# The first batch pair's loads, tail block and bias in a hand-scheduled attention and MLP-mixer kernel

## The chip, the cores and the metric

The kernel runs on one core of a Trainium2 chip. The metric is device microseconds of one execution; less is better. The core's TensorE (PE, with its weight loads PEld), VectorE (DVE), ScalarE (ACT), GpSimd (POOL) and SyncE (SP) run side by side, each its own instructions in order, and wait for each other by semaphores. Sixteen DMA engines move data; POOL, SP and ACT issue the transfers.

## What is computed

For 8 batches, 8 heads, 576 positions and a head width of 64:

```python
scores = (q @ k.T) / 8 - slopes[h] * abs(i - j)         # masked unless 0 <= i - j < 128
x      = softmax(scores) @ v                            # heads side by side: (8, 576, 512)
h      = relu(x.T @ w_tok1) @ w_tok2                    # 576 -> 256 -> 576, over positions
u      = x + h.T
out    = u + relu(u @ w_ch1) @ w_ch2                    # 512 -> 1536 -> 512, over channels
```

All arrays are float32 in memory. The kernel works in bf16 with float32 sums; the POOL loads convert on the way.

## The kernel before

**Blocks and pairs.** The 576 positions of a batch are 4 blocks of 128 and a rest of 64 (R). Batches go in pairs. A pair has 9 blocks: 0 to 3 are the first batch, 4 to 7 the second, and block 8 (TAIL) holds both rests, the first batch's in partitions 0 to 63 and the second's in 64 to 127. Because of the window of 128 a block looks only at itself and the block before it.

**Stages.** `side(b)` does batch b's attention and its token mixing. For each block: `transposes` (q and k of a block to `qkT`, on PE by L644 with a copy by L650, or later in the kernel as a DMA transpose by L633), `scores` (L684; then exp on ACT, L707; then the product with a mask on DVE, L717), `values` (L750; then reciprocal L763 and normalization L766). Then `token_mix`: L795 and L805 (the tail's share) into relu (L813), L838/L841 back to positions, the sum `ub` (L853, L856), and its transpose `uT` (L873 with copy L879, or a DMA transpose). `main(b)` does the channel mixing: `chunk` (L1035: one of 12 pieces of the hidden width, four matmuls of 512 columns, then relu L1041), `tail_piece` (L1078), and the second product. In every batch `second` (L1212) forms that product by seven half-sized products, which share three accumulation banks: products 1, 6, 7, 4 in one bank, 5 and 3 in another, 2 in the third. Product 6 waits until the result of 1 has been taken out of the bank (L1183), 7 until that of 6, 4 until that of 7, and 3 until that of 5. The tail block's second product is L1123. `main(b)` is interleaved with `side(b+1)`.

**Bias.** Two ways to bring in the slope term and the mask exist. For a block listed in `BIASED` (and of the first pair's first batch) PE adds them before the scores: `bias` (L693), two groups of four matmuls with a diagonal matrix `slant`, 128 columns wide for block 0 and 256 for others. Then DVE does not multiply by a mask. All other blocks use the mask products (L717), two to a block. `TURNED` makes the bias of a block other than 0 wait for that block's transposes.

**What sets the order.** The program is straight-line. `Plan` holds every operation with an engine, a cost and a rank, and `Plan.run` plays them through a model at build time; each engine then gets its operations in the order that came out, once and for all. `SEEDS[part]` adds a random shift of up to 1500 to the ranks of one part (part 0 is the first `side`, part b+1 is `main(b)` with `side(b+1)`); zero leaves the ranks as they are. `HALF` is a rate of the model alone. With `SECOND_LATE` the first matmuls of products 1, 2 and 5 may not be placed before the last scores of the interleaved `side`. `emit` fills PE's planned gaps in the first 60 us with matmuls of zeros (L1268), whose results nobody reads. Nothing of this runs on the chip but its order.

**Loads.** Block 0's q and k come by SP and ACT (L484). All others of the first pair and all weights are issued by POOL in the order of the string `LOADS`: `q2` is q of block 2, `W1` is w_tok1 with the first copy of its rest, `P0` the second copy of that rest, `W2` and `T0` are w_tok2, `A0` to `A3` are quarters of w_ch1 (hidden pieces 0-2, 3-5, 6-8, 9-11), `B0` to `B3` quarters of w_ch2. `load` issues one DMA for a block (128 rows by 8 heads) and, for the tail, one of 64 rows by 8 heads for each batch. A model of eight slots limits how many are under way. The later pairs' loads follow in the order of use; they wait for a free `qk` or `v` buffer (five of each).

**The tail of the first pair.** `q8`, `k8` and `v8` load only the first batch's 64 rows; the other 64 rows of these buffers are zeroed beforehand by L542 and L543. The second batch's rows come later as `lk8`, `lq8` and `lv8`, which rewrite the lower half (`rewrites`, `later`, `slot`): they wait for the first users of the buffer. `side` therefore transposes the tail twice in the first pair, once for each batch.

**Start of the first channel mixing.** In `main(0)` the first `PIECES` pieces of the hidden width are formed block by block (L1020, four matmuls of 128 columns for each block and piece), so that they can begin before all blocks of `uT` are there. Each piece holds a PSUM bank of the four that transposes, values and token mixing use as well.

Of the kernel before, what the change touches and what calls it, by code (L numbers as in the profile page):

```python
# [20 lines left out]
class Buf:  # L21
    def __init__(self, ring, choice):
        self.ring, self.choice, self.slot = ring, choice, None
        self.writers, self.parts, self.users, self.later = [], {}, [], []

    def __call__(self):
        got = self.ring.slots[self.slot[0]]
# [38 lines left out]
class Plan:  # L66
# [6 lines left out]
    def buf(self, name, choice=None):  # L73
        return Buf(self.rings[name], choice or self.rings[name].each)

    def op(self, eng, cost, emit, rank, makes=(), adds=(), rewrites=(), part=None, uses=(), reads=(), needs=(),
           after=0.0, order=None, bus=0.0, other=None, mode=0, behind=()):
        def many(x):
            return list(x) if isinstance(x, (list, tuple)) else [x]

        o = Op()
        o.eng, o.cost, o.emit, o.rank, o.after, o.part = eng, cost, emit, rank, after, self.part
        o.t0 = o.done = None
        o.order, o.bus, o.other, o.mode = order, bus, other, mode
        o.n = len(self.ops)
        o.deps = set(many(needs))
        o.behind = list(behind)
        o.bufs = []
        for b in many(makes):
            b.writers.append(o)  # L90
            o.bufs.append(b)
        for b in many(adds):
            o.deps.update(b.writers)
            b.writers.append(o)
            o.bufs.append(b)
        for b in many(rewrites):
            o.deps.update(u for u in b.users if u not in b.later)
            b.later.append(o)
            b.writers.append(o)
            o.bufs.append(b)  # L100
        if part is not None:
            b, key = part
            b.parts.setdefault(key, []).append(o)
            o.bufs.append(b)
        for b in many(uses):
            o.deps.update(b.writers)
            o.bufs.append(b)
        for b, key in many(reads):
            o.deps.update(b.parts[key])
            o.bufs.append(b)  # L110
        o.deps.discard(o)
        for b in o.bufs:
            b.users.append(o)
        self.ops.append(o)
        return o

    def slot(self):
        self.orders += 1
        return self.orders

    def dma(self, emit, descs, packets, makes=(), rewrites=(), order=None, uses=()):
        o = self.op("POOL", 550 + 0.33 * descs, emit, 0, makes=makes, rewrites=rewrites, uses=uses,
                    order=order or self.slot())
        o.packets = packets
        return o

    def run(self):
        ops = self.ops
        dice = [random.Random(x) for x in SEEDS]
        for o in ops:  # L130
            if SEEDS[o.part]:
                o.rank += dice[o.part].uniform(-SHIFT, SHIFT)
# [177 lines left out]
    def emit(self, spin):  # L310
# [12 lines left out]
        for _, _, go in sorted(work, key=lambda w: w[:2]):  # L323
# [3 lines left out]
WARM = 6500.0  # L327
FIRST = -5e5
GRACE = 0.4
PIECES = 2  # L330
HOLD = 3
FROM_QK = 10
FROM_U = 2
# [4 lines left out]
MERGEM = 9  # L338
MERGES = 9
FAST = range(8)  # L340
PRODUCTS = [1, 5, 6, 2, 3, 7, 4]
RANKT = 0
RANKS = 0
RANKH = 0
RELU = 350
SUMS_AT = 60e3
SEEDS = [63488, 544433, 0, 603260, 673561, 0, 172207, 0, 0]
SHIFT = 1500.0
UNIT_LATE = True
SECOND_LATE = False  # L350
BIASED = [0, 1, 2]
THIRD = [(4, 5)]
TURNED = False
SLANT = 4.0e3
HALVED = 2
BANKS = 8
# [6 lines left out]
STORE = 774.0  # L363
TURN = [(792.0, 1267.0), (1380.0, 2400.0)]
RATES = [(0.37, 0.23), (0.52, 0.35), (0.47, 0.18)]
HALF = 0.7
EARLY = 1


LOADS = ("q2 k1 q1 v1 k2 k3 v0 q3 v2 v8 W1 q8 k8 v3 W2 k6 k5 q5 k4 q6 A0 q4 "  # L370
         "v4 lk8 lq8 k7 A1 q7 v5 A2 B0 v6 A3 v7 lv8 B1 B2 T0 P0 B3")


@with_exitstack
def kernel(
# [16 lines left out]
    P = nc.NUM_PARTITIONS  # L392
    B, H, S, D = q.shape
# [5 lines left out]
    R = S - NC * P  # L399
    NB = 2 * NC + 1  # L400
    TAIL = 2 * NC
# [16 lines left out]
    plan = Plan()  # L418
# [36 lines left out]
    W1 = const.tile([P, NC, DTOK], BF16, name="W1")  # L455
    W1p = const.tile([P, 2, DTOK], BF16, name="W1p")
    W2 = const.tile([P, NJ, NC * P], BF16, name="W2")
# [12 lines left out]
    def rows(t, b, s0, n):  # L470
        return t[b, :, s0 : s0 + n, :].rearrange("h s d -> s h d")

    def parts_of(pr, blk):
        if blk == TAIL:
            return [(2 * pr + i, NC * P, R, i * R) for i in range(2)]
        return [(2 * pr + blk // NC, (blk % NC) * P, P, 0)]

    pe_, act_, dve_ = nc.tensor, nc.scalar, nc.vector
# [27 lines left out]
    def block(pr, blk):  # L506
        if (pr, blk) not in held:
            held[pr, blk] = {"qk": plan.buf("qk"), "v": plan.buf("v")}
        return held[pr, blk]

    def load(name, pr, blk, parts, order=None):
        got = block(pr, blk)
        buf = got["v" if name == "v" else "qk"]
        src = {"q": q, "k": k, "v": v}[name]

        def to():
            return buf()[:, :, 0:D] if name == "v" else buf()[:, "qk".index(name), :, :]

        for b, s0, n, p0 in parts:
            def go(b=b, s0=s0, n=n, p0=p0):  # L520
                nc.gpsimd.dma_start(out=to()[p0 : p0 + n, :, :], in_=rows(src, b, s0, n))  # L521
            kw = {"makes": buf} if order is None else {"rewrites": buf, "order": order}
            plan.dma(go, n * H, 1024 if n == P else 520, **kw)

    def weights(parts):
        return [plan.dma(lambda o=o, i=i: nc.gpsimd.dma_start(out=o, in_=i), n, s) for o, i, n, s in parts]
# [6 lines left out]
    for i_, name in enumerate("qk"):  # L533
        raw = raws[i_]
        buf = block(0, 0)["qk"]
        plan.op("DVE", 480, lambda raw=raw, buf=buf, i="qk".index(name): dve_.tensor_copy(
            out=buf()[:, i, :, :], in_=raw.rearrange("p (h d) -> p h d", h=H)), -100 + i_, makes=buf, after=4.75e3 + 600 * i_)
    if PADT:
        for i in range(2):
            plan.op("DVE", 190, lambda i=i: dve_.memset(W1p[(1 - i) * R : (2 - i) * R, i, :], 0.0), -90)  # L540
    last = block(0, TAIL)
    plan.op("DVE", 180, lambda b=last["qk"]: dve_.memset(b()[R:P, :, :, :], 0.0), -90, makes=last["qk"])  # L542
    plan.op("DVE", 180, lambda b=last["v"]: dve_.memset(b()[R:P, :, 0:D], 0.0), -90, makes=last["v"])  # L543
    lw1, lw2, lw2t, lc1, lc2, later = [], [], [], [], [], []
    for item in LOADS.split():
        what, n = item[:-1], int(item[-1])
        if what in ("q", "k", "v"):
            load(what, 0, n, parts_of(0, n)[0:1])
        elif what in ("lq", "lk", "lv"):
            later.append((what[1], plan.slot()))  # L550
        elif what == "W":
            if n == 1:
                lw1 += weights([(W1[:, 0:NC, :], w1, 512, 2080)] +
                               [(W1p[0:R, 0, :], moe_w_tok1[NC * P : S, :], 64, 420)])
            else:
                lw2 += weights([(W2[:, :, :], w2[:, :, 0 : NC * P], 256, 2630)])
        elif what == "P":
            lw1 += weights([(W1p[R:P, 1, :], moe_w_tok1[NC * P : S, :], 64, 420)])
        elif what == "T":
            lw2t += weights([(W2t[:, :, :], w2[:, :, NC * P : S], 256, 300)])  # L560
        elif what == "A":
            hs = slice(n * DCH // 4, (n + 1) * DCH // 4)
            lc1 += weights([(WC1[:, :, hs], c1[:, :, hs], 512, 2500)]) * (NHT // 4)
        else:
            js = slice(n * NHT // 4, (n + 1) * NHT // 4)
            lc2 += weights([(WC2[:, js, :], c2[:, js, :], 384, 2680)]) * (NHT // 4)
# [52 lines left out]
    qkT, xbs, ubs, r1s, uts, wides = {}, {}, {}, {}, {}, []  # L619
# [267 lines left out]
    def side(b, rank):  # L887
        pr, half = b // 2, b % 2
        if half == 0:
            xbs[pr], ubs[pr] = plan.buf("xb"), plan.buf("ub")  # L890
        if pr < HALVED:
            units = list(range(half * NC, (half + 1) * NC)) + [TAIL]
        else:
            units = [[0, 1, 2, 3, TAIL], [4, 5, 6, 7]][half]
        prev = None
        for u in units + [None]:
            if u is not None:
                need = [u, 2 * NC - 1] if u == TAIL and pr >= HALVED else [u]
                for w in need:
                    if (pr, w) not in qkT or (u == TAIL and pr == 0):  # L900
                        transposes(pr, w, rank(0 if by_transfer(pr, w) else 450))
                hf = half if u == TAIL and pr < HALVED else None
                pb = scores(pr, u, hf, rank(450), wides if b == 1 else ())
            if prev is not None:
                values(pr, prev[0], prev[1], prev[2], rank)
            prev = None if u is None else (u, hf, pb)
        token_mix(b, rank)
# [99 lines left out]
    def main(b, rank):  # L1007
# [6 lines left out]
        if b == 0:  # L1014
            first = [bank() for _ in range(PIECES)]
            for blk in blocks:
# [132 lines left out]
    def second(b, rank, r2, ss, sums, ub):  # L1149
# [53 lines left out]
        DONE = {1: (0, 0, False), 5: (1, 1, False), 6: (0, 1, False), 7: (1, 1, True), 2: (0, 0, True), 3: (0, 1, True), 4: (1, 0, True)}  # L1203
        for m in PRODUCTS:
            l, w, s, tt = L[m]
# [39 lines left out]
    SIDE = [[5 * 930 + 5 * 480, 5 * 930 + 5 * 480], [5 * 930 + 6 * 450, 4 * 930 + 3 * 450]]  # L1245
    base = 0.0
    side(0, along(-1e6, 1.0, 1.0))
    for name, order in later:
        load(name, 0, TAIL, parts_of(0, TAIL)[1:2], order)
    for b in range(B):  # L1250
        n = LEN[b % 2]
        plan.part = b + 1
# [49 lines left out]
```

## Time and profile before

| what | value |
|---|---|
| median of 3 runs (279.9 to 280.82) | 280.22 us |
| profiled execution | 280.18 us |
| its span, first to last instruction | 278.0 us |
| PE busy in the span | 270.4 us, 2871 matmuls |
| DVE, ACT, POOL busy | 210.0, 136.2, 116.3 us |
| matmuls of zeros L1268 | 73, the last at 24.6 us |
| bias matmuls L693 | 24 (8 of 128 columns, 16 of 256), 3.6 to 11.7 us |
| transposes by PE L644 | 88 matmuls, 5.7 to 56.4 us |
| POOL issues of q, k, v L521 | 118, about 0.88 us each for 128 rows |
| granted TensorE clock | 1.00 throughout |

The span is the profile's own clock; 2.2 us of the execution lie around it. Of a matmul the profile shows a modelled end, so that neighbours overlap and a busy PE says little; the distance from start to start is what counts, and the chain of waits shows it: it books each group of matmuls until the next one starts. "x8" after a line is the number of instructions of a group, and what stands in brackets is how long the engine was idle before it and what ended that. For a POOL load the duration is the issuing; "DMA to landing" runs from the start of the issue until the data is there.

### The profile page before, as it was taken

Reading aid. Unit: us, or ns where it says so; the run is one execution under the profiler, and the core shown is the slowest. Engines: PE = TensorE matmul, PEld = TensorE weight load, DVE = VectorE, ACT = ScalarE, POOL = GpSimd, SP = SyncE. Lnnn points to the kernel's source line nnn. Section 1 sums busy time; section 2 is a strip of 40 time slices with the busy share of each in tenths; the row PEclk is TensorE's granted clock in tenths of the full one; section 3 lists DMA queues with packets and bytes.
Section 4 is the critical chain, followed back from the end, with each engine's and each line's share of the span. In section 5 each row is a group of like instructions: output and inputs, shape, how many; then the busy total and the mean of one; then the engine's idle time right before and its main releaser. Section 6 shows DMA issues by size and latency. Waiting matters only on the chain.

```text
span 278.0 us, 7069 instructions
## 1 busy us (share of the span) xinstructions
PE 270.4 (97%) x2871; PEld 181.7 (65%) x2871; DVE 210.0 (76%) x486; ACT 136.2 (49%) x216; POOL 116.3 (42%) x146
## 2 busy tenths in 40 slices
PE   7989999999999999999999999999999999999994
PEld 4865755676686546595667655586666755489983
DVE  8467799968897569964898469862978569877972
ACT  5563996336970298007860087206951077215500
POOL 8998848940382018900594008800480320022000
PEclk9999999999999999999999999999999999999999
DMA  9999999999599689999999999979799930052014
GB/s 132 151 159 170 191 191 179 156 140 232 73 127 154 137 211 128 132 136 202 174 137 158 201 174 75 146 123 207 136 135 112 171 134 2 8 142 98 2 59 130
DMA packets 167535, 38.43 MB, mean 138 GB/s; under 512 B 155792, under 2 KB 166672, under 8 KB 167504
## 3 DMA queue, kind: packets, MB, share of 16 engines
q0 software_dynamic: 116112, 20.03, 92.5%
q1 hardware_dynamic: 50352, 17.70, 31.6%
q8 instruction: 22, 0.36, 0.5%
q10 hardware_dynamic: 1040, 0.26, 0.4%
q14 instruction: 9, 0.07, 0.1%
HBM read 35.85 MB, written 9.44 MB: 163 GB/s over the span
## 4 chain that ended last, share of the span: by engine, by line
PE 85%; DVE 6%; POOL 4%; DMA 2%; issue 0%; ACT 0%; POOLq 0%
PE ps L1212 25%; PE ps L1035 24%; PE ps L750 6%; PE ps L684 6%; PE ps L838 4%; PE ps L795 4%; PE ps L1078 4%; PE ps L1123 4%; PE ps L957 3%; POOL qk L521 2%; DMA v<-in_v_dram 2%; DVE s L1060 1%; POOL v L521 1%; PE ps L644 1%; DVE WT L582 1%; PE ps L873 1%
## 5 line engine op out<-in xcount | busy, mean ns | idle before, releaser
L1035 PE MATMUL ps<-uT,WC 128*128 128x512 bf16 x328 | 79.5, 379 | 0.0
L1041 ACT ACTIVATE r<-ps 128x512 bf16<-128x512 f32 x75 | 44.3, 602 | 57.4 <-PE ps L1035 52.9
L707 ACT ACTIVATE pe<-ps 128x1024 bf16<-128x1024 f32 (+1 forms) x76 | 63.5, 888 | 18.1 <-PE ps L684 17.7
L521 POOL DMA_DIRECT2D v<-in_v_dram x40 | 34.4, 862 | 89.9 <-PE ps L750 88.2
L1035 PEld LDWEIGHTS <-WC 128*128 128x128 bf16 x328 | 29.1, 98 | 28.3
L717 DVE TENSOR_TENSOR pe<-pe,mask 128x1024 bf16<-128x1024 bf16 (+1 forms) x62 | 37.1, 607 | 8.0 <-ACT pe L707 7.3
L1212 PEld LDWEIGHTS <-r 128*128 128x128 bf16 x384 | 36.9, 98 | 7.9 <-issue 0.7
L521 POOL DMA_DIRECT2D qk<-in_q_dram x39 | 34.0, 877 | 2.8 <-PE ps L750 1.4
L521 POOL DMA_DIRECT2D qk<-in_k_dram x39 | 34.1, 883 | 2.1 <-DMA v<-in_v_dram 1.1
L1212 PEld LDWEIGHTS <-s 128*128 128x128 bf16 x288 | 27.5, 98 | 6.3 <-issue 1.8
L766 DVE TENSOR_TENSOR xb<-ps,rt 128x256 bf16<-128x256 f32 (+1 forms) x73 | 29.5, 419 | 0.8
L750 PEld LDWEIGHTS <-pe 128*128 128x128 bf16 (+1 forms) x560 | 21.6, 100 | 9.6 <-DVE pe L717 2.6
L750 PE MATMUL ps<-v,pe 128*128 128x65 bf16 (+1 forms) x560 | 26.2, 194 | 1.2 <-DMA v<-in_v_dram 1.2
L1212 PE MATMUL ps<-WC,r 128*128 128x256 bf16 x192 | 25.4, 273 | 0.0
L1212 PE MATMUL ps<-WT,s 128*128 128x256 bf16 x192 | 24.2, 273 | 0.0
L1212 PE MATMUL ps<-WT,r 128*128 128x256 bf16 x192 | 23.7, 273 | 0.0
L1183 DVE TENSOR_TENSOR ob<-ps,ub 128x512 f32<-128x512 f32 x22 | 15.2, 689 | 10.1 <-PE ps L1212 10.0
L856 DVE TENSOR_TENSOR ub<-ps,xb 128x512 bf16<-128x512 f32 x34 | 21.4, 684 | 1.4 <-PE ps L838 1.2
L684 PEld LDWEIGHTS <-qkT 64*128 64x128 bf16 x560 | 14.8, 94 | 10.9 <-issue 9.7
L763 DVE RECIPROCAL rt<-ps 128x4 f32<-128x4 f32 (+1 forms) x76 | 12.3, 175 | 10.1 <-PE ps L750 9.4
L684 PE MATMUL ps<-qkT 64*128 64x128 bf16 (+1 forms) x304 | 19.4, 216 | 0.0
L838 PE MATMUL ps<-r,W 128*128 128x512 bf16 x64 | 16.1, 379 | 0.1
(96 smaller groups left out, 336.4 us busy)
## 6 DMA issues: line engine op xcount, KB each, us to landing
out_dram<-ob SPq DMA_DIRECT2D x17, 256.0 KB, 2.5
v<-in_v_dram POOLq DMA_DIRECT2D x32, 128.0 KB, 4.8
qk<-in_q_dram POOLq DMA_DIRECT2D x31, 128.0 KB, 4.9
qk<-in_k_dram POOLq DMA_DIRECT2D x31, 128.0 KB, 4.8
WC<-in_moe_w_ch_dram POOLq DMA_DIRECT2D x8, 384.0 KB, 9.0
out_dram<-raw SPq DMA_DIRECT2D x7, 256.0 KB, 2.6
out_dram<-ob POOLq DMA_DIRECT2D x5, 256.0 KB, 2.9
out_dram<-raw POOLq DMA_DIRECT2D x3, 256.0 KB, 3.0
```

The lines of the kernel that those rows point to most:

```text
L521: nc.gpsimd.dma_start(out=to()[p0 : p0 + n, :, :], in_=rows(src, b, s0, n))
L684: pe_.matmul(wide(e)[:, i, kind, a:z], lhsT=ts[kb]()[e * D : (e + 1) * D, NHP + i, :], rhs=ts[blk]()[e * D : (e + 1) * D, i, a:z], start=n ...
L707: act_.activation(out=pb()[:, e, :, lo:, c0:c1_], in_=wide(e)[:, :, lo:, c0:c1_], func=ACT.Exp, scale=scale)
L717: dve_.tensor_tensor(out=o, in0=o, in1=heads(mk, es), op=ALU.mult)
L750: pe_.matmul(view()[a:z, at, i, :], lhsT=pb()[:, e, i, kind, a:z], rhs=vb()[:, h, 0 : D + 1], start=m == 0, stop=m == len(mms) - 1, skip_g ...
L766: dve_.tensor_tensor(out=x4(), in0=view()[r0:r1_, :, :, 0:D], in1=rt()[r0:r1_, 0:n, :, :].broadcast_to([r1_ - r0, n, 4, D]), op=ALU.mult)
L838: pe_.matmul(ht()[:, hs], lhsT=W2[:, j, c * P : (c + 1) * P], rhs=r1()[:, j, :], start=j == 0, stop=j == NJ - 1 and not fold)
L856: plan.op("DVE", 690, lambda blk=blk, ht=ht, hs=hs: dve_.tensor_tensor(out=ub()[:, blk, :], in0=ht()[:, hs], in1=xb()[:, blk, :], op=ALU.a ...
L1035: pe_.matmul(ct()[:, :], lhsT=WC1[:, cb, t * P : (t + 1) * P], rhs=uT()[:, cb, :], start=cb == 0, stop=cb == NCB - 1)
L1041: plan.op("ACT", 600, lambda t=t, ct=ct: act_.activation(out=r2()[:, t, :], in_=ct()[:, :], func=ACT.Relu), rk, part=(r2, t), uses=[ct], o ...
L1183: dve_.tensor_tensor(out=v, in0=bk().rearrange("p (c n) -> p c n", c=2), in1=src, op=ALU.add)
L1212: pe_.matmul(bk()[:, c * HN : (c + 1) * HN], lhsT=l(t, c), rhs=w(t), start=first, stop=g == 1 and t == HK - 1, skip_group_check=True)
```

## The change

The second batch's half of the first pair's tail is no longer loaded apart: `q8`, `k8` and `v8` each issue both halves, one behind the other. The memsets, the rewriting loads and the second transposing of the tail go. PE forms the bias of block 0 only; blocks 1 and 2 are masked by DVE. The first-pair loads and the weights are issued in another order. Three instead of two pieces of the hidden width are begun block by block. In the second product 7 comes before 3, in all batches. `SECOND_LATE` and `TURNED` are switched on, `HALF` is another number, and other parts have their ranks shifted.

```diff
-    def op(..., makes=(), adds=(), rewrites=(), part=None, ...):
+    def op(..., makes=(), adds=(), part=None, ...):
...
-        for b in many(rewrites):
-            o.deps.update(u for u in b.users if u not in b.later)
-            b.later.append(o)
-            b.writers.append(o)
-            o.bufs.append(b)
...
-PIECES = 2
+PIECES = 3
...
-PRODUCTS = [1, 5, 6, 2, 3, 7, 4]
+PRODUCTS = [1, 5, 6, 2, 7, 3, 4]
...
-SEEDS = [63488, 544433, 0, 603260, 673561, 0, 172207, 0, 0]
+SEEDS = [554399, 0, 0, 0, 0, 0, 0, 0, 399558]
...
-SECOND_LATE = False
-BIASED = [0, 1, 2]
+SECOND_LATE = True
+BIASED = [0]
...
-TURNED = False
+TURNED = True
...
-HALF = 0.7
+HALF = 0.9
...
-LOADS = ("q2 k1 q1 v1 k2 k3 v0 q3 v2 v8 W1 q8 k8 v3 W2 k6 k5 q5 k4 q6 A0 q4 "
-         "v4 lk8 lq8 k7 A1 q7 v5 A2 B0 v6 A3 v7 lv8 B1 B2 T0 P0 B3")
+LOADS = ("v0 k1 q1 v1 q3 q2 k2 W1 k3 v2 q8 k8 k5 v3 v8 W2 k6 q6 A0 q5 k4 q4 "
+         "A1 A2 q7 k7 v6 v5 P0 v4 B0 T0 A3 v7 B1 B2 B3")
...
-    last = block(0, TAIL)
-    plan.op("DVE", 180, lambda b=last["qk"]: dve_.memset(b()[R:P, :, :, :], 0.0), -90, makes=last["qk"])
-    plan.op("DVE", 180, lambda b=last["v"]: dve_.memset(b()[R:P, :, 0:D], 0.0), -90, makes=last["v"])
...
         if what in ("q", "k", "v"):
-            load(what, 0, n, parts_of(0, n)[0:1])
-        elif what in ("lq", "lk", "lv"):
-            later.append((what[1], plan.slot()))
+            load(what, 0, n, parts_of(0, n))
...
-                    if (pr, w) not in qkT or (u == TAIL and pr == 0):
+                    if (pr, w) not in qkT:
                         transposes(pr, w, rank(0 if by_transfer(pr, w) else 450))
...
-    for name, order in later:
-        load(name, 0, TAIL, parts_of(0, TAIL)[1:2], order)
```

More of the change, by code (lines that the diff above doesn't have):

```diff
@@ L23, in __init__ @@
         self.ring, self.choice, self.slot = ring, choice, None
-        self.writers, self.parts, self.users, self.later = [], {}, [], []
+        self.writers, self.parts, self.users = [], {}, []
     def __call__(self):
@@ L74, in buf, with op @@
         return Buf(self.rings[name], choice or self.rings[name].each)
-    def op(self, eng, cost, emit, rank, makes=(), adds=(), rewrites=(), part=None, uses=(), reads=(), needs=(),
+    def op(self, eng, cost, emit, rank, makes=(), adds=(), part=None, uses=(), reads=(), needs=(),
            after=0.0, order=None, bus=0.0, other=None, mode=0, behind=()):
@@ L115, in op, with dma @@
         return o
-    def slot(self):
+    def dma(self, emit, descs, packets, makes=(), uses=()):
         self.orders += 1
[L119 to L123, printed above, removed]
+        o = self.op("POOL", 550 + 0.33 * descs, emit, 0, makes=makes, uses=uses, order=self.orders)
         o.packets = packets
@@ L509, in block, with load @@
         return held[pr, blk]
-    def load(name, pr, blk, parts, order=None):
+    def load(name, pr, blk, parts):
         got = block(pr, blk)
@@ L521, in go @@
                 nc.gpsimd.dma_start(out=to()[p0 : p0 + n, :, :], in_=rows(src, b, s0, n))
-            kw = {"makes": buf} if order is None else {"rewrites": buf, "order": order}
-            plan.dma(go, n * H, 1024 if n == P else 520, **kw)
+            plan.dma(go, n * H, 1024 if n == P else 520, makes=buf)
     def weights(parts):
@@ L540 @@
             plan.op("DVE", 190, lambda i=i: dve_.memset(W1p[(1 - i) * R : (2 - i) * R, i, :], 0.0), -90)
-    last = block(0, TAIL)
-    plan.op("DVE", 180, lambda b=last["qk"]: dve_.memset(b()[R:P, :, :, :], 0.0), -90, makes=last["qk"])
-    plan.op("DVE", 180, lambda b=last["v"]: dve_.memset(b()[R:P, :, 0:D], 0.0), -90, makes=last["v"])
-    lw1, lw2, lw2t, lc1, lc2, later = [], [], [], [], [], []
+    lw1, lw2, lw2t, lc1, lc2 = [], [], [], [], []
     for item in LOADS.split():
```

## The prediction

> **What bounds the kernel now.** I read the page first: busy times and the chain that ended last.
>
> ```profile
> PE 270.4 (97%) x2871; PEld 181.7 (65%) x2871; DVE 210.0 (76%) x486; ACT 136.2 (49%) x216; POOL 116.3 (42%) x146
> ...
> PE 85%; DVE 6%; POOL 4%; DMA 2%; issue 0%; ACT 0%; POOLq 0%
> ```
>
> PE carries the end, but a busy PE is no proof of a full one. So next I asked for the windows of two stretches: from batch 3's first L1035 to batch 4's, and from batch 5's to batch 6's (places from the chain of waits).
>
> ```profile
> 125.87:159.42 33.55, 33.55 (x356) 21.69 (x354) 24.21 (x54) 16.21 (x24) 13.65 (x16) 1.00 1.50 171
> 186.30:220.74 34.44, 34.44 (x372) 22.58 (x370) 24.19 (x54) 16.92 (x25) 10.72 (x13) 1.00 1.18 148
> ```
>
> The second column is the length. The second stretch has 16 more matmuls, one L1078 group, which the chain books at 0.89 us: 33.55 + 0.89 = 34.44. So the same work takes the same time to 0.01 us, though the two parts have differently shifted ranks (seeds 673561 and 172207). Once PE is fed, the order is worth nothing here; what counts is when PE becomes full and how much work it has.
>
> When it becomes full is in the chain of waits, 0 to 31 us (start, us, what):
>
> ```profile
> 8.74 1.57 POOL v L521 x2
> 10.31 0.75 POOL W L526
> 11.06 0.54 POOL W1p L526
> 11.61 1.30 POOL qk L521 x2
> 12.91 5.86 DMA v<-in_v_dram
> 18.77 0.04 issue
> 18.81 0.40 PE ps L750 x8
> ...
> 19.73 0.34 PE ps L684 x16
> 20.07 0.66 PE ps L1268 x7
> 20.73 0.86 PE ps L795 x4
> 21.59 0.37 PE ps L750 x8
> ...
> 22.66 0.75 PE ps L795 x3
> 23.41 0.55 PE ps L805 x2
> ```
>
> For 12.9 us the chain is little but POOL issuing loads. The fifteenth transfer, v3, is the last that batch 0 needs; it lands at 18.77. The tail's scores (L684) stand behind v3's values (L750) on PE, then come exp, mask, tail values and L805 at 23.41: 4.64 us after v3. From about 25 us there are no more matmuls of zeros. **Everything before is start-up, and the change is nearly all there.**
>
> **The change, part by part.**
>
> *Loads in front of the last one needed (moved).* Before v3 POOL issued 9 full loads, 3 halves (v8, q8, k8) and W1 in two. After, before v3: v0 k1 q1 v1 q3 q2 k2 k3 v2 k5, 10 full, 4 halves (q8 and k8 whole) and W1; then both halves of v8. Prices: a full load's issue is 0.87 (8.74 to 10.31 is a full and a half, 1.57, so a half 0.70), and between landings a full one is 0.84 in the trace (k1, q1, v1 land at 7.08, 7.93, 8.80), a half 0.42 (lk8, lq8 land 0.42 apart at 28.33 and 28.75) to 0.59 (q8). So v3 moves by 0.87 + 0.70 = 1.57 in issue, by 0.84 + 0.42 = 1.26 in landing at the least. I take 1.45, between the two: v3 at 20.2. v8's second half is two halves later, 21.1, which is 2.3 after the load that was last before.
>
> How much of it arrives at L805? Lower end: if the tail's scores come before v3's values on PE, what is left after v3 is L750 twice with normalization (18.81 to 20.73 less the 0.34 of scores and 0.66 of zeros, about 0.9), eight L795 (1.73), the tail values (0.74) and waits: L805 near 23.7, +0.3. Upper end: the whole 2.3. I take the row nearest to it, the same order as before: v3's 1.45 passes whole, and v8 at 21.1 is hidden, since the tail values would start at 21.59 + 1.45. **+1.45**; ends +0.3 and +2.3. Nothing fills the hole: q6 and k6, the next work, are loaded later still.
>
> *Tail turned once (removed).* The second transposing of the tail falls in the time in which PE is full; the chain of waits prices transposes there:
>
> ```profile
> 27.62 0.89 PE ps L644 x16
> ```
>
> Two sets are 0.89, one 0.45: **-0.45**. With it go one copy L650 (0.69 on DVE or 1.01 on ACT) and two memsets (0.49 and 0.27), beside PE: 0; if ACT or DVE were late for the next set, up to 0.4 more gain.
>
> *Bias of blocks 1 and 2 gone, masks come.* From the list of line L693:
>
> ```profile
> L693 PE MATMUL ps<-WS x24: 216/272/421, 3.6 to 11.7; 128*128 128x256 bf16 x16, 128*128 128x128 bf16 x8
> ```
>
> The 16 of 256 columns go: 16 x 0.109 (L1212's rate, 0.66 for six) = 1.74 us of PE, at 8.7 to 12.0 us, where PE waits for loads and multiplies zeros. So 0; all 1.74 only if loads were no bound. In exchange DVE gets four masks L717 of 0.69, 2.7 us, between 10 and 20 us, where the windows show it busy 3.39 + 3.05 of 10. Hidden by the wait for v3; without that cover the last pair, 1.4, would stand in the chain.
>
> *PIECES 3.* Sixteen matmuls of 128 (0.89, L1078's row) instead of four of 512 (0.86): **+0.03**. One more bank is held from about 28.6 to 31.7. Ends: a gain of 0.86, if PE lacked work there, and a loss of 1.0, if a transposing waits out a copy L650 for a bank. I take 0 beyond the 0.03, by the two equal stretches.
>
> *Later loads.* W1's and W2's places aside, the sum is the same: the second halves of the tail are only moved. From v8 at 21.1, with A and B quarters at 1.9 (A0 landed 1.92 after q6, A1 1.89 after k7): A2 comes near 31.8 instead of 35.2, v4 near 36.7 instead of 27.9, v7 near 41.5 instead of 40.8, B3 near 47.3, as before. The first values of batch 1 ran at 35.6 anyway, so v4 hides behind chunks; A2 early gains nothing on a full PE. DVE is 4.93 of 5 busy from 40 us; it loses a copy and gains nothing. 0; ends -0.5 and +0.8 (v7).
>
> *No wait is added on POOL.* The rewriting loads waited for the tail's first users, finished long before (POOL's waits name none of it).
>
> *Product 7 before 3; SECOND_LATE; seeds.* 7 waits for the eviction of 6 (L1183, 0.69), covered by product 2 (1.31), and 3 now covers the one between 7 and 4, which L1123 covered at the end. In the timeline all products but one group (batch 1, 77.5 us, scores until 79.3) start after the last scores anyway. By the equal stretches 0 each; ends -0.3 and +0.7, one eviction at the very end. TURNED cannot act, since the one block left in BIASED is 0; HALF is the planner's alone.
>
> **Sum**: 1.45 - 0.45 + 0.03 = +1.03 on the profiled execution's 280.18 us: **281.2 us**. That execution and the median of the runs shown (280.22) differ by 0.04.
>
> **A rule that speaks against it.** PE's early pace is in the timeline of its weight loads:
>
> ```profile
> 1.60 0.15 PEld L1268 LDWEIGHTS <-zero 128*128 128x128 bf16 x1 [0.28 <-issue]
> 2.02 0.15 PEld L1268 LDWEIGHTS <-zero 128*128 128x128 bf16 x1 [0.28 <-issue]
> 2.45 0.15 PEld L1268 LDWEIGHTS <-zero 128*128 128x128 bf16 x1 [0.28 <-issue]
> ```
>
> One matmul of 512 columns in 0.42 us, where L795 later takes 0.216 (four in 0.86): half pace, although the granted clock reads 1.00. Before, PE's longest wait for data was 1.18 us, at v3, and the pace held. The Trainium skill, "TensorE: Matmul & The Clock Gate", Part 1, says that the array starts at half clock, gets the full one after about 3.4 us of activity, and loses it after about as long idle. The early pace agrees with it; no run here shows the loss.
>
> **Rivals.**
>
> 1. *Slower still: PE goes back to half pace.* Decides if the plan expects v3 and v8 too early, so that PE stands still, with no zeros planned, for far longer than the 1.18 before: 1.18 + 2.3 = 3.5 us is the most these rows give. Then v8's 2.3 passes whole, and the next work runs at half pace for as long as at the start (1.2 to 2.9 us, 1.7, of which half is lost, 0.85): 2.3 + 0.85 - 0.45 + 0.03 = +2.7, **282.9**. For it: v3 did come later than planned. Against it: zeros are spread through all the start-up.
>
> 2. *No change: hidden.* The tail's scores get ahead of v3, L805 at +0.3: 0.3 - 0.45 + 0.03, **280.1**. For it: q8 and k8 now come two transfers ahead of v3, not one.
>
> 3. *Faster: the transfers catch up.* Between v2 (13.04) and v3 (18.77) lie 5.73 us, while the rows give 3 x 0.42 + 1.12 (W1) + 0.21 + 0.84 = 3.43. The other 2.3 us are two jumps, at v8 and v3. If half loads on the lower partitions alone cause them, whole tails don't have them: v3 then lands 2.3 earlier than forecast and L805 comes at +1.45 - 2.3 = -0.85, sum -1.27, **278.9**. Against it: q8 and k8 are such halves too and show 0.59 and 0.46. The Trainium skill, "DMA: Bandwidth & Descriptors", section on why a DMA increments its semaphore by 16, spreads 64 partitions over all 16 engines, which would leave no such cause; no view here shows the engines apart.
>
> 4. *It does nothing*, if blocks 1 and 2 still had the bias or the tail two transposings: excluded by the diff.
>
> **Chances.** Forecast 0.45 (280.6 to 282.1 with its inner spread; about 0.12 of it is under the bound). Rival 1, or v8's delay passing whole without it: 0.17. Rival 2: 0.19. Rival 3: 0.19. What can be told from no change is 0.3%, 0.84 us: faster means under 279.4, slower over 281.06. Faster 0.19 (rival 3), same 0.19 + 0.12 = 0.31, slower 0.33 + 0.17 = 0.50. The range runs from rival 3's 278.9 to rival 1 plus a late last eviction, 282.9 + 0.7: 278.9 to 283.6; outside it lie rival 3 with gains of its own, and a PE starved in the middle.
>
> **What would show it.** v3's issue near 14.5 and landing near 20.2; v8's second half near 21.1; L805 near 24.9. L644 80 matmuls, L693 8, L1020 48, 66 masks L717 instead of 62. The two stretches above as long as before. Wrong, if L805 stands at 23.7 or earlier and the time doesn't move, if the stretches differ (then order matters), or if PE waits over 2 us after 20 us.

## The result, and the profile after

The changed kernel takes 281.67 us (280.81 to 282.52) beside 280.36 us (279.9 to 280.85) for the kernel before: a ratio of 1.0049, 95% interval 1.003 to 1.0068, that is 1.31 us more, by the interval 0.8 to 1.9. One of the nine executions of the changed kernel took 348.38 us at a granted clock of 0.754; the range and the ratio leave it out. The forecast was 281.2. The profiled execution took 281.92 us with a span of 280.1, 1.74 and 2.1 more than before.

Lines move up by 15 in most places: L644 is now L629, L684 L669, L717 L702, L750 L735, L805 L790, L1035 L1020, L1020 L1005, L1078 L1063, L1212 L1197, L1268 L1251.

The same two lines of the page, busy times and the chain by engine:

```profile
PE 273.7 (98%) x2894; PEld 184.3 (66%) x2894; DVE 211.3 (75%) x487; ACT 134.3 (48%) x219; POOL 115.7 (41%) x146
...
PE 91%; DMA 3%; DVE 3%; ACT 1%; issue 0%
```

POOL has left the chain, and 3.3 us of PE have been added although the change takes PE work away. The chain of waits of the start (start, us, what) says what was added:

```profile
17.74 0.55 PE ps L669 x16
18.30 0.35 PE ps L735 x8
18.64 0.45 PE ps L629 x8
19.09 1.04 PE ps L1251 x10
20.13 0.34 PE ps L669 x16
20.47 0.44 PE ps L1251 x6
...
22.97 0.22 PE ps L1251 x2
23.19 1.73 PE ps L780 x8
24.91 0.53 PE ps L790 x2
```

L790, the tail's token mixing, stands at 24.91 where 24.9 was forecast (before: L805 at 23.41). But no load is in this chain. From 6.2 us on it is PE alone, and of the 18.08 us from 6.83 to 24.91 the matmuls of zeros (L1251) take 9.01, the sum of their rows. In the kernel before, added up from the PE timeline between 6.6 us and L805, zeros take 4.5 us and waits 1.25. v3 was issued at 14.22 (forecast 14.5) and landed at 18.36, not at 20.2: 0.4 us *earlier* than before. v8's last rows landed at 19.94 instead of 21.1. PE waited for neither. Behind the wait for the first zeros (1.2), the list of PE's waits has only these (us in total, times, longest; the last is the first block's, at 6 us):

```profile
PE ps L1020 <- DMA uT<-ub: 0.4, 1, 0.4
PE ps L735 <- DVE xb L751: 0.3, 1, 0.3
PE ps L629 <- DVE qk L526: 0.3, 1, 0.3
```

The counts are those forecast: L629 80, L678 8, L1005 48, L702 66 masks. The two stretches of the middle, between the same places, are as long as before (34.44 with three groups of the tail piece, L1063):

```profile
126.90:161.40 34.50, 34.48 (x371) 22.73 (x372) 24.04 (x54) 16.66 (x25) 13.65 (x16) 1.00 1.56 167
189.60:224.00 34.40, 34.40 (x373) 22.63 (x371) 24.14 (x54) 16.66 (x25) 12.14 (x15) 1.00 1.18 158
```

So the number came out and the cause did not: the transfer did not come late, PE did. Three accounts are tested from here. Theory A: PE's own stream, made long by zeros, sets the start, and the rest is how well one written-out order happens to fit the chip. Rival B, the prediction's: the places of the loads set it. Rival C: a single edit (SECOND_LATE, the bias, the whole tail, the products) carries the 1.3 us.

### The profile page after: what moved, and what is told of

It is laid out like the page before. It is cut to its first block, busy times and chain, and to the rows that moved or that the text cites. A ratio compares the mean times of both kernels' runs of the same rounds, so it can differ in the third digit from the quotient of the medians.

```text
span 280.1 us, 7151 instructions
## 1 busy us (share of the span) xinstructions
PE 273.7 (98%) x2894; PEld 184.3 (66%) x2894; DVE 211.3 (75%) x487; ACT 134.3 (48%) x219; POOL 115.7 (41%) x146
## 4 chain that ended last, share of the span: by engine, by line
PE 91%; DMA 3%; DVE 3%; ACT 1%; issue 0%
PE ps L1197 25%; PE ps L1020 24%; PE ps L735 7%; PE ps L669 6%; PE ps L780 5%; PE ps L823 5%; PE ps L1063 4%; PE ps L1108 4%; PE ps L1251 3%; PE ps L942 3%; PE ps L629 2%; DMA uT<-ub 2%; DMA raw<-in_k_dram 2%; PE ps L790 1%; DVE pe L702 1%; PE ps L1005 1%
## 5 line engine op out<-in xcount | busy, mean ns | idle before, releaser
L1020 PE MATMUL ps<-uT,WC 128*128 128x512 bf16 x324 | 78.6, 379 | 0.4 <-DMA uT<-ub 0.4
L702 DVE TENSOR_TENSOR pe<-pe,mask 128x1024 bf16<-128x1024 bf16 (+1 forms) x66 | 39.8, 613 | 13.2 <-ACT pe L692 12.3
L1020 PEld LDWEIGHTS <-WC 128*128 128x128 bf16 x324 | 28.5, 98 | 29.1 <-issue 0.9
L1197 PEld LDWEIGHTS <-r 128*128 128x128 bf16 x384 | 36.9, 98 | 6.6 <-issue 1.3
L1197 PEld LDWEIGHTS <-s 128*128 128x128 bf16 x288 | 27.7, 98 | 6.0 <-issue 1.7
L735 PEld LDWEIGHTS <-pe 128*128 128x128 bf16 (+1 forms) x560 | 21.3, 100 | 8.1 <-DVE pe L702 2.2
L735 PE MATMUL ps<-v,pe 128*128 128x65 bf16 (+1 forms) x560 | 26.0, 194 | 0.3 <-DVE xb L751 0.3
L1197 PE MATMUL ps<-WC,r 128*128 128x256 bf16 x192 | 24.6, 273 | 0.0
L1197 PE MATMUL ps<-WT,s 128*128 128x256 bf16 x192 | 23.6, 273 | 0.0
L1197 PE MATMUL ps<-WT,r 128*128 128x256 bf16 x192 | 23.6, 273 | 0.0
L669 PEld LDWEIGHTS <-qkT 64*128 64x128 bf16 x560 | 14.9, 95 | 11.7 <-issue 10.6
L669 PE MATMUL ps<-qkT 64*128 64x128 bf16 (+1 forms) x304 | 19.6, 218 | 0.0
L1180 POOL DMA_DIRECT2D out_dram<-ob x5 | 3.6, 725 | 36.2 <-DVE ob L1168 36.2
L1168 DVE TENSOR_TENSOR ob<-ps,ub 128x512 f32<-128x512 f32 x20 | 13.8, 689 | 4.3 <-PE ps L1197 4.3
L1168 DVE TENSOR_TENSOR ob<-ps,ob 128x512 f32<-128x512 f32 x16 | 11.0, 691 | 7.4 <-PE ps L1197 7.4
```

The costliest lines, as they stand in the source:

```text
L669: pe_.matmul(wide(e)[:, i, kind, a:z], lhsT=ts[kb]()[e * D : (e + 1) * D, NHP + i, :], rhs=ts[blk]()[e * D : (e + 1) * D, i, a:z], start=n ...
L702: dve_.tensor_tensor(out=o, in0=o, in1=heads(mk, es), op=ALU.mult)
L735: pe_.matmul(view()[a:z, at, i, :], lhsT=pb()[:, e, i, kind, a:z], rhs=vb()[:, h, 0 : D + 1], start=m == 0, stop=m == len(mms) - 1, skip_g ...
L1020: pe_.matmul(ct()[:, :], lhsT=WC1[:, cb, t * P : (t + 1) * P], rhs=uT()[:, cb, :], start=cb == 0, stop=cb == NCB - 1)
L1168: dve_.tensor_tensor(out=v, in0=bk().rearrange("p (c n) -> p c n", c=2), in1=src, op=ALU.add)
L1197: pe_.matmul(bk()[:, c * HN : (c + 1) * HN], lhsT=l(t, c), rhs=w(t), start=first, stop=g == 1 and t == HK - 1, skip_group_check=True)
```

## The experiments

**SECOND_LATE off.** `SECOND_LATE = True` becomes `False`, nothing else.

> The changed kernel with SECOND_LATE off again, nothing else. The prediction priced it at 0: the products stand behind the last scores anyway, and once PE is fed the order is worth nothing; then 281.7 us, within 0.4, and the stretches of batches 3 and 5 keep their 34.4 us. Rival: the order is worth nothing only between two orders that both work; without this rule products 1, 2 and 5 take PSUM banks that the scores of the next batch need, PE stands idle while ACT and DVE catch up, and the time is 284 us or more. The first 20 us are the changed kernel's own, so they also show whether its slow early pace (weight loads 0.42 us apart at 8 us) comes back in another execution or was chance: if chance, transposes of block 1 at 8.2 us instead of 9.2.

Measured: 296.59 us, ratio 1.0621 (1.0574 to 1.0667): 14.9 us above the changed kernel. The windows of its trace show where (the columns are length, then PE, PEld, DVE, ACT and POOL busy, granted clock, DMA share, GB/s):

```profile
90.00:100.00 10.00, 6.47 (x93) 4.58 (x95) 7.74 (x21) 5.47 (x8) 5.96 (x7) 0.66 1.03 86
100.00:110.00 10.00, 3.42 (x23) 1.57 (x22) 4.32 (x10) 0.60 (x1) 1.94 (x3) 0.83 1.18 114
```

The second products of batch 1 were all placed by 88.8 us, ahead of batch 2's attention. That attention then ran bare: scores, exp, mask and values one after the other, with nothing on PE beneath them. The chain of waits shows one block of it:

```profile
88.83 0.60 PE ps L669 x16
89.43 1.02 ACT pe L692
...
90.47 0.70 DVE pe L702
...
91.22 0.42 PE ps L735 x8
```

In these two windows the changed kernel's PE is busy for 10.00 and 9.96 us. The next question was whether the switch is worth this, or the switch without an order made for it.

**SECOND_LATE off, with other shifts.** Part 0 keeps its shift, so the start is the same.

```diff
-SECOND_LATE = True
-SEEDS = [554399, 0, 0, 0, 0, 0, 0, 0, 399558]
+SECOND_LATE = False
+SEEDS = [554399, 462319, 430422, 412632, 431053, 0, 147326, 0, 330692]
```

> The changed kernel with SECOND_LATE off, like the first of these experiments, but with other shifts of the ranks in the parts from main(0) on (the start, part 0, keeps its own). Theory (the switch and the seeds fit each other, the switch by itself is worth nothing): the 15 us that turning the switch off had cost go away, 281 to 283 us, and PE is busy through batch 2's attention between 85 and 115 us. Rival (the switch itself is worth 15 us, since it keeps second products back to lie under the scores): 294 to 298 us whatever the shifts are.

Measured: 282.35 us, ratio 1.0078 (1.0052 to 1.0103). Of the 14.9 us, 14.2 go with nothing but other shifts. What is left for the switch as such is 0.7 us, less than two orders of the same work differ by (next run); the order around it is worth 14.

**Shifts alone.** All nine shifts other, the work the same.

```diff
-SEEDS = [554399, 0, 0, 0, 0, 0, 0, 0, 399558]
+SEEDS = [572764, 512577, 184918, 431151, 626093, 240344, 233136, 423338, 11064]
```

> The changed kernel with other shifts of the ranks in all parts, nothing else: the work is the same, only the order in which the engines get it differs. It measures how much a second tuned order scatters, which the runs with new shifts need. Theory (between tuned orders the order is worth nothing, as the prediction's equal stretches say): 281.7 us within 0.6. Rival (orders that count as equally good still differ by more than that on the chip): 282.5 us or more, or under 281.

Measured: 282.87 us, ratio 1.0105 (1.0076 to 1.0133), clear of the changed kernel's interval, so the rival holds: these two tuned orders of the same work differ by 1.2 us by the medians. L790 came at 24.14, 0.8 us *earlier* than in the changed kernel's chain; the gain was lost behind it. One such place is in its waits:

```profile
PE ps L942 <- DVE tt L906: 1.4, 1, 1.4
```

This stands at 252.4 us, in the last batch, and the trace of the changed kernel has no such wait. From here on, 1.2 us is the least that a run with new shifts must differ by before an edit can be blamed. That holds for the change too: it came with new shifts, and its 1.3 us are hardly more than that.

**No zeros after 11 us.** `FILL = 60000.0` becomes `11000.0` in the changed kernel: gaps planned later stay empty.

> The changed kernel without the matmuls of zeros whose planned gap begins after 11 us. Theory of the prediction (the loads set the start): v3 and v8 set the token mixing's end, L790 stays at 24.9 us, the zeros' place is idle, 281.7 us. Theory after the traces (PE's own stream sets it: it runs late from 9 us on, and zeros fill every planned gap, so that it can't catch up): with the gaps free PE catches up, L790 at 22.5 to 23.5, time 1.4 to 2.0 us less, 279.7 to 280.3. Third: without zeros PE falls to half pace, 512 columns again take 0.42 us after 15 us, and the time is 282.5 or more.

Measured: 280.72 us, ratio 1.0027 (1.0004 to 1.005), so 0.95 us less than the changed kernel by the medians, 0.6 by the ratios; the intervals overlap, so the gain in time alone is not proof. The trace is plainer: in the timeline, from which L790 is given from here on, L790 starts at 23.44, where the changed kernel has 24.85 (0.6 of that is early pace, see below). The two lines, the changed kernel's first:

```profile
24.85 0.60 PE L790 MATMUL ps<-xb,W1p 64*128 64x512 bf16 x2
23.44 0.60 PE L790 MATMUL ps<-xb,W1p 64*128 64x512 bf16 x2
```

PE now waits for a load again:

```profile
20.85 0.67 PE L735 MATMUL ps<-v,pe 128*64 128x65 bf16 x16 [0.96 <-DMA v<-in_v_dram]
```

This is v8's last half, landed at 20.71. So beneath the zeros a load was still a bound, but v8's, not v3's, and 0.8 to 1.4 us further down.

**The same in the kernel before.** `FILL = 60000.0` becomes `11000.0` there.

> The kernel before, without the zeros that are planned after 11 us. Theory (zeros cost time only where PE is late against the order written down for it and waits for no load; in the kernel before PE stands still 1.18 us for v3 at 18.8 us): 0 to -0.3 us, 280.1 to 280.4. Rival (zeros cost the same in both kernels, some 0.95 us): 279.4 us.

Measured: 282.12 us, ratio 1.0058 (1.004 to 1.0077): *slower* by 1.6 us by the ratio, which neither theory had. Windows of this trace:

```profile
15.00:18.50 3.50, 1.94 (x42) 1.39 (x38) 2.53 (x7) 2.95 (x3) 3.50 (x5) 0.99 1.79 157
18.50:21.80 3.30, 3.30 (x30) 1.44 (x29) 2.07 (x7) 1.08 (x2) 3.30 (x5) 0.50 2.41 154
```

and of the changed kernel without late zeros, the same two stretches:

```profile
15.00:18.50 3.50, 2.11 (x56) 1.68 (x56) 3.43 (x9) 2.31 (x3) 3.50 (x6) 1.00 2.20 140
18.50:21.80 3.30, 1.67 (x44) 1.34 (x38) 2.57 (x10) 1.16 (x3) 3.30 (x5) 1.00 1.42 130
```

The third number from the end of a line is the granted clock. With PE busy for 1.94 of 3.50 us the clock fell to 0.50 for the next 3.3 us, just after v3 had landed (17.82) and PE had full work; half of that, 1.65 us, is lost. In the other kernel's trace PE was as idle, and the clock stayed. The mean granted clock of every execution says how often. In seven of the eight executions here it is 0.990 to 0.994; in all of the kernel before it is 0.996 to 1.00. In the changed kernel without late zeros two of the ten have 0.990 and 0.994 (281.27 and 281.87 us), the others 0.997 or more. So zeros do hold the pace, but whether a gap loses it differs from one order to the other and from one execution to the next. That the 1.6 us are this loss fits in size and is not shown: the profiled execution, which lost the pace, is the fastest of the eight (280.87 us) with L805 at 23.07 (23.37 in the kernel before), and the only one that kept the clock took 280.99.

**Zeros kept up to v3, dropped behind it.** `FILL = 17200.0` in the kernel before. In the trace of the kernel before 17 zeros stand behind that, 5 at 19.1, 7 at 20.0, 5 at 24.4 us.

> The kernel before without the zeros planned after 17.2 us (in the trace of before 17 matmuls: 5 at 19.1, 7 at 20.0, 5 at 24.4 us, about 0.9 us). Theory (zeros before v3 hold the full pace, those after it only stand in the way of late work, since PE is busy without them): 0.5 to 0.9 us less, 279.3 to 279.7. Rival 1 (they hold the pace too, as those between 11 and 17 us did): slower, 281 us or more. Rival 2 (the lost time is made up elsewhere): 280.1 us.

Measured: 279.72 us (278.98 to 280.59), ratio 0.9984 (0.9971 to 0.9997). The direction is the theory's, and the size, 0.54 us by the medians and 0.45 by the ratio, is at the lower edge of its band. L805 stands at 23.30 (before 23.37) although v3 landed at 19.00 here, 0.23 later than in the first trace. It is the only version found that is ahead of both kernels, by less than 0.3%.

**The loads in the old order.** The changed kernel with before's `LOADS`, q8, k8 and v8 whole.

```diff
-LOADS = ("v0 k1 q1 v1 q3 q2 k2 W1 k3 v2 q8 k8 k5 v3 v8 W2 k6 q6 A0 q5 k4 q4 "
-         "A1 A2 q7 k7 v6 v5 P0 v4 B0 T0 A3 v7 B1 B2 B3")
+LOADS = ("q2 k1 q1 v1 k2 k3 v0 q3 v2 v8 W1 q8 k8 v3 W2 k6 k5 q5 k4 q6 A0 q4 "
+         "v4 k7 A1 q7 v5 A2 B0 v6 A3 v7 B1 B2 T0 P0 B3")
```

> The changed kernel with the loads in the order of before, the tail whole at the places of q8, k8, v8. If the change's order of loads costs the 1.45 us that the prediction gave it, L790 comes back to about 23.5 to 24.3 (the three second halves remain in front, 3 x 0.42 = 1.26) and the time falls to about 281. If PE's own stream sets the start, the old order gains nothing: v3 has 3 halves more in front than before, and the tail's chain hangs behind it; L790 at 24.9 or later, 281.7 to 283.

Measured: 283.11 us, ratio 1.0103 (1.0053 to 1.0153), 1.4 us above the changed kernel, L790 at 25.61, v3 landed at 19.49. So the old order of the loads does not undo the loss. With the whole tail the new order is the better of the two, but the intervals overlap, and the shifts here were made for the new one.

**v3 right behind v2.** The changed kernel, v3 and v8 ahead of k5, other shifts.

```diff
-LOADS = ("... v2 q8 k8 k5 v3 v8 W2 ...
+LOADS = ("... v2 v3 q8 k8 v8 k5 W2 ...
-SEEDS = [554399, 0, 0, 0, 0, 0, 0, 0, 399558]
+SEEDS = [685077, 0, 131363, 659495, 442107, 237609, 592915, 599681, 0]
```

> The changed kernel with v3 issued right behind v2, ahead of q8, k8 and k5, and v8 ahead of k5, with shifts chosen anew. Prediction's step (v3's landing passes whole to L790): v3 lands some 2.5 us earlier than in the changed kernel's trace, and L790 comes 0.4 to 1.5 us earlier, near 23.4 to 24.4 us, so 280.2 to 281.3. Rival (in the changed kernel PE waits for no load after 6 us; its own stream with the zeros in it sets the start): v3 earlier, L790 between 24.5 and 25.3 us as before, 281.3 to 282.3.

Measured: 283.11 us, ratio 1.0106 (1.0087 to 1.0125). v3 landed at 16.30, 2.06 earlier than in the changed kernel; L790 (here L789) came at 23.87 instead of 24.85, 0.98 earlier. That lies in the prediction's band, but the trace with SECOND_LATE off, which has the changed kernel's loads and start, shows L790 at 24.25: against that it is 0.4. So the start favours B a little and settles nothing, and none of it reached the end: PE waits twice, at 188 and at 252 us, for the transpose of the tail.

```profile
PE ps L1062 <- DMA uTt<-ub: 2.2, 2, 1.1
```

**The whole tail alone.** Before's constants, with the tail loaded whole and transposed once (the code of the change).

> The kernel before with the tail loaded whole at q8, k8, v8 and turned once; bias, pieces, seeds, products and order as before. By the prediction's prices: three halves more in front of v3, +1.26, one transposing less, -0.45: +0.8, 281.2 us. If the transfers catch up with whole tails as in the changed kernel (v2 to v3 3.98 us instead of 5.73), v3 lands no later than before and the time is 279.9 or less. If the start and the order after it must fit each other (PE's stream is planned), it costs more than the loads: 282 or more.

Measured: 281.89 us, ratio 1.0072 (1.0043 to 1.0101): the tail whole, without the rest of the change, costs 1.5 us by the medians, 2.0 by the ratio. L805 (here L790) came at 24.19, 0.8 later, with v3 landed at 19.88, 1.1 later. Here PE does wait for v3, as the prediction had it for the change:

```profile
19.92 0.40 PE L735 MATMUL ps<-v,pe 128*128 128x65 bf16 x8 [0.78 <-DMA v<-in_v_dram]
```

So rival C is not excluded: this part of the change costs as much as the whole, though no more than shifts alone may. The missing transposing (-0.45) is not seen as a gain; the shifts here are those made for the tail in halves.

**The bias back, in two orders.** `BIASED = [0, 1, 2]`, `TURNED = False` in the changed kernel, with two sets of shifts.

```diff
-BIASED = [0]
-TURNED = True
-SEEDS = [554399, 0, 0, 0, 0, 0, 0, 0, 399558]
+BIASED = [0, 1, 2]
+TURNED = False
+SEEDS = [281285, 0, 525373, 193002, 264378, 155394, 356620, 181219, 22777]
```

> The changed kernel with the bias of blocks 1 and 2 by TensorE again (16 matmuls of 256 columns, 1.74 us) in place of four masks on VectorE, TURNED off as before, and shifts of the ranks chosen anew for it. Theory (the bias only takes the place of zeros that PE multiplies in the start anyway): 281 to 282.3 us, zeros L1251 some 1.5 us fewer, L790 within 0.6 us of the changed kernel's 24.9. Rival (PE is full from the start, as its chain has it): 1.74 us more, 283.4 us, and L790 near 26.5.

Measured: 283.24 us, ratio 1.0107 (1.0075 to 1.0138). L790 at 23.75, *earlier* than the changed kernel's 24.85, and 19 zeros fewer (89 for 108). That start does not pay for the bias, though the time does fit the rival's 283.4. So a second order was run, `SEEDS = [604205, 0, 356181, 0, 674663, 149528, 0, 0, 399558]`:

> The changed kernel with the bias of blocks 1 and 2 by TensorE again, as in the run before with new shifts, but with yet other shifts. That run was 1.6 us slower than the changed kernel although its start was earlier. Theory (the bias is free in the start, and the 1.6 us came from the order behind it): 281.3 to 282.3 us. Rival (the 1.74 us of bias do pass into the end): 283.2 us again.

Measured: 281.66 us, ratio 1.0053 (1.0036 to 1.0071), the changed kernel's own time. The same edit reads +1.6 in one order and 0.0 in the other (L790 at 24.64, 0.2 earlier). The bias of blocks 1 and 2 costs nothing that shows above what orders differ by.

**Product 7 before 3 in the kernel before.** `PRODUCTS = [1, 5, 6, 2, 7, 3, 4]`.

> The kernel before with product 7 ahead of 3, nothing else. Prediction's term: 0, so 280.4 us within 0.4, the last eviction at the end included. Rival (each single piece of a tuned order is worth microseconds once PE's order shifts, as SECOND_LATE was): 282 us or more.

Measured: 280.17 us, ratio 1.0003 (0.998 to 1.0025): nothing, as forecast. Its profiled execution was the longest of its twelve (282.07): there W1 landed at 17.58 instead of 15.59, one transfer's jump that the first trace of the same loads does not have at that place.

## Why the prediction was right, and where it was not

**v3 moves by 1.45 and passes whole: the step that failed, in both halves.** *v3 lands at 20.2*: it landed at 18.36. Nor was that one lucky execution. Four traces with before's loads have v3 at 17.82, 18.77, 19.00 and 19.29 (mean 18.7); seven with the change's loads at 18.36, 18.42, 18.79, 18.80, 18.97, 19.57 and 19.62 (mean 18.9). Issued 1.3 us later or more, it lands 0.2 later. Between v2 and v3 pass 4.5 to 6.1 us in the first four and 3.4 to 4.0 in the other seven: rival 3's catching up is real, and it goes with the order of the loads. Its cause in rival 3, half loads on the lower partitions, falls: in the kernel before with the tail whole the same gap is 6.9 us, 1.3 of it for three more half loads. *And PE waits for it*: no, although it does with the tail whole in the kernel before (0.78 us). What put L790 at 24.91 were the 9.01 us of zeros, written into gaps at build time and multiplied whether PE was early or late. Where something delays PE, zeros keep it from catching up; without them L790 came 1.4 earlier, 0.8 earlier than with zeros and quick early pace. Nor is the place itself +1.45 when like is compared with like, for the early pace (next paragraph) was quick in the profiled execution of the kernel before and slow in the changed one's. Quick in both, it is 24.25 (SECOND_LATE off, the same start) against 23.37; slow in both, 24.85 and 24.90 against 23.90 (the run with product 7 first): 0.9 to 1.0 later. That 24.9 and 281.2 were met is luck.

**What delayed PE.** Part of it is early pace. The timeline of weight loads, first of the changed kernel:

```profile
7.94 0.13 PEld L1251 LDWEIGHTS <-zero 128*128 128x128 bf16 x2 [0.20 <-issue]
8.35 0.15 PEld L1251 LDWEIGHTS <-zero 128*128 128x128 bf16 x1 [0.28 <-issue]
8.78 0.47 PEld L1251 LDWEIGHTS <-zero 128*128 128x128 bf16 x4 [0.28 <-issue]
```

then of the kernel with SECOND_LATE off, whose start is the same instruction for instruction:

```profile
6.92 0.71 PEld L1251 LDWEIGHTS <-zero 128*128 128x128 bf16 x7
8.67 0.45 PEld L629 LDWEIGHTS <-qk 128*128 128x128 bf16 x8 [1.03 <-DMA qk<-in_q_dram]
```

0.42 us from one 512-column matmul to the next is half pace; the second trace has the full one. Of four traces with this start two are slow until some 10 us and two are quick by 6 us; of the four with the start of the kernel before two are slow at 8.5 us and two are not. It is the execution, not the change. In the two slow traces L790 is at 24.85 and 24.90, in the quick one with zeros at 24.25, so it is worth 0.6 there.

**Tail turned once, -0.45.** The 8 transposes went, but the gain cannot be seen: the whole tail alone cost 1.5 us, and 0.8 of that already stands at L790.

**Bias 0, PIECES 3 +0.03, later loads 0.** The bias holds within the orders' difference (+1.6 and 0.0). The later transfers came near to forecast (A2 at 32.7 for 31.8, v4 37.2 for 36.7, v7 42.5 for 41.5, B3 47.8 for 47.3), and PE's only wait among them is 0.28 us for DVE at 40.3. PIECES was not tried alone.

**Products, SECOND_LATE and seeds 0 each, "by the equal stretches".** Right for the products (1.0003). For the change as a whole it held too: all the stretches are equal. As a rule it was wrong. Equal stretches show that two good orders run alike in those stretches. They do not show that an order may be disturbed for nothing: one switch without shifts to match is worth 14.9 us, and two good orders of the same work 1.2 us.

**Rival 1, back to half pace.** It did not happen in the traces of the change, with or without the late zeros, but the mechanism, which no trace of before showed, is real: see the last section. Its price rested on a misread start: in the kernel before seven zeros of 128 columns take 0.74 us from 2.88 on and six take 0.33 from 6.63 on, so the half pace did not end at 2.9. **Rival 2**, hidden, is what the change without its late zeros nearly is: 280.72. **Rival 3** had the transfers nearly right (v3 at 17.9 for 18.36) and the end wrong.

**What stays open.** Zeros hold some 0.6 to 0.95 of the 1.3 us, by intervals that overlap. The rest, what the whole tail costs apart from the order, and why two tuned orders differ by 1.2 us, were not followed to their ends; every order has its own late waits (1.4 us in the last batch in one, 2.2 at two tail transposes in another), and a tail transposing saved is lost among them. Why transfers jump where they do was not found.

## What to carry to other kernels

Before you charge a late transfer to the end, look for filler in front of the consumer: matmuls that only fill planned gaps are executed as fixed work, so here they hid a transfer that came early and kept an engine that was late from catching up. Keep filler where idle time would cost the pace, up to the last load that the engine must wait for, and drop it behind that (279.72 against 280.26 us).

In a kernel whose order is written out as a whole, undoing one edit does not price the edit: here 14.9 us for a switch became 0.7 with a fresh order. Find out first what a fresh order alone does (here 1.2 us), and believe no price below that.

## What the runs showed of the hardware

**Loss of pace.** With SECOND_LATE off, PE stood idle for 5.85 us before L1020 at 109.8. The weight loads behind that (timeline) are 0.43 us apart, and full pace is back after 113.2, 3.4 us later:

```profile
112.77 0.15 PEld L1020 LDWEIGHTS <-WC 128*128 128x128 bf16 x1 [0.28 <-issue]
113.20 0.61 PEld L1020 LDWEIGHTS <-WC 128*128 128x128 bf16 x3 [0.28 <-issue]
114.23 0.45 PEld L669 LDWEIGHTS <-qkT 64*128 64x128 bf16 x16 [0.42 <-issue]
```

The Trainium skill, "TensorE: Matmul & The Clock Gate", Part 1, gives both lengths as a window of some 3.4 us that runs free of the program; here the trace agrees (5.85 us idle, 3.4 us at half pace). A free-running window alone does not explain the early pace: with the same instructions it ends by 4.3 us in one execution and at 10.0 in another, further apart than one such window.

**Loss without an idle window.** In the kernel before without zeros after 11 us, PE's longest waits between 15 and 18.5 us were 0.98 us (for q8) and 0.57 us (for v3), and it was busy for 1.94 of 3.50 us; the pace was lost all the same, for 3.3 us. The table in the Trainium skill, "TensorE: Matmul & The Clock Gate", Part 1, gives one idle window of about 3.4 us for the loss; here the measurement decides: a half-busy one sufficed, and in another kernel's trace it did not (2.11 of 3.50, then 1.67 of 3.30 us, clock 1.00).

**Transfers in jumps.** With the same loads, issued at the same times, W1 landed at 15.59, 15.84, 17.24 and 17.58 us in four executions, and v3 up to 1.5 us apart.
